# Top-k attention with an MLP behind it: the heads of pairs 1 to 3 loaded by rows and turned on TensorE

## The chip, the cores and the metric

The kernel runs on one core of a Trainium2 chip. The metric is device time in microseconds (us); a time given for a kernel is the median of several runs. One execution of each kernel is also recorded by the hardware profiler; that record is the profile, or the trace. Its engines are TensorE (PE; its weight loads are PEld), VectorE (DVE), ScalarE (ACT), GpSimd (POOL) and SyncE (SP), which here only issues DMAs. ACTq and SPq are DMA issues on the queues of ScalarE and SyncE. An entry such as L331 is a line of the kernel's source.

## The reference

Eight batches of eight heads, 576 positions, 64 values a head, all float32. Each row of scores keeps its 32 largest; the rest is masked out before the softmax. The heads' outputs side by side are the rows x (512 wide) of an MLP with a normalization ahead of it and a residual. The weights arrive as float64, and the kernel converts them to float32 itself.

```python
# attention: q, k, v are (8, 8, 576, 64)
scores = (1 / sqrt(64)) * q @ k^T
kth    = 32nd largest of each row of scores
scores = where(scores >= kth, scores, -1e9)
attn   = softmax(scores);  o = attn @ v
# MLP: x is (8, 576, 512), w_ch1 (512, 2048), w_ch2 (2048, 512)
xn  = (x - mean(x)) / sqrt(var(x) + 1e-6) * g_ln
out = x + relu(xn @ w_ch1) @ w_ch2
```

## The kernel before

**Tiling.** A job is one batch, one pair of heads (two heads of 64 fill the 128 partitions) and a group of query tiles. A query tile is 128 rows; the 576 rows are four whole tiles and a rest of 64. A unit is one query tile of a job for both heads: its scores are 128 x 2 x 576. The first jobs are batch 0 with its pairs 0, 1, 2, 3 and query tiles 0 and 1, so job 0 has units 0 and 1, job 1 has units 2 and 3, and so on; the next four jobs are the same pairs with query tiles 2 and 3. The list `fresh` holds the jobs that meet a batch and pair for the first time; the others get the turned heads back from a copy in DRAM (`keep_heads` stores it, `fetch_heads` loads it).

**Turned heads.** The scores need k and q with the 64 values of a head on the partitions and positions along the row: kT (128 x 576), qT (128 x 256, query tiles 0 and 1) and late_qT (128 x 320, the others). `load` brings k and q so that VectorE's transpose, which works on blocks of 32 x 32, ends in that layout: four DMAs for k and four for q, each with runs of 32 floats, 128 bytes. `turn_heads` (L331) then makes three VectorE transposes. k and q each have a tile of their own (`kin`, `qin`), in a pool with one buffer, so the next job's load waits until these are turned.

**The order.** There are 160 units, and the program is written out step by step; in step n VectorE selects the top values of unit n (four rounds of MAX8 and MATCH_REPLACE8, L447 and L433; `select`) and halves the next unit (L425, L426; `halve`), TensorE makes the scores of unit n + 2 (L404), ScalarE copies them out of PSUM (L385; `take_scores`), ScalarE and GpSimd mask unit n - 1 (L496, then the subtraction L499) and ScalarE takes the exponential (L507). In the first eight steps TensorE then turns that unit's weights in two halves (L565, copied out by ScalarE in L577) and an end piece (L599, L609). A group's values follow (L632, L640; `values`), and `place` puts them into x (L677, L654). Every engine works through its own instructions strictly in program order. A list `todo` holds the MLP's matmuls; each step takes from it in several `fill()` calls what its share allows. The MLP begins at step 9, with its first product on TensorE at 109.7 us.

**The weights.** A piece is 128 x 512 float64, fetched by SyncE (L147) into one of four buffers. ScalarE splits it in three instructions (L163, L165, L168), GpSimd clamps the size and scales the sign (L164, L170), VectorE shifts (L176), and GpSimd joins (L182, L184). Four pieces are split before step 0, then one a step up to step 7 and two a step from step 10.

**Where heads are turned.** The main loop holds a table `turns`: job 1 is turned in step 0, job 2 in step 1, job 3 in step 2, and the next fresh job, of batch 1, in step 12 (its first transpose is at 143.7 us). In a step the turn stands after VectorE's second selection round, and between the first and second half of the unit's turn on TensorE; the load of the next fresh job follows it at once:

```python
        if n in turns:
            turn_heads(turns[n])
            later = fresh.index(turns[n]) + 1
            if later < len(fresh):
                load(fresh[later], nc.sync, nc.sync, n >= EARLY)
        if n == 0:
            scores(units[2])
            take_scores(units[2])
```

Ahead of step 0 stands a start-up: job 0 is loaded and turned, unit 0 scored, job 1 loaded with k on SyncE's queue and q on ScalarE's, unit 1 scored and copied, the norm's gain g brought into place by a small TensorE transpose (L196, copied by L197), and four pieces split. PSUM has eight banks: five for the attention's short results (`brief`) and three for the MLP's products (`product`).

Of the kernel before, what the change touches and what calls it, by code (L numbers as in the profile page):

```python
# [11 lines left out]
FP32 = mybir.dt.float32  # L12
# [9 lines left out]
J = 4  # L22
# [7 lines left out]
def compute(  # L30
# [12 lines left out]
    nc = tc.nc  # L43
    P = nc.NUM_PARTITIONS
    B, H, S, D = q.shape
# [3 lines left out]
    JP = J * P  # L49
    R = S - JP  # L50
    NHP = H // 2
# [5 lines left out]
    def pool(name, bufs, **kw):  # L57
        return ctx.enter_context(tc.tile_pool(name=name, bufs=bufs, **kw))
# [6 lines left out]
    ldpool = pool("ld", 1)  # L65
# [24 lines left out]
    def const(shape, name):  # L90
        return consts.tile(shape, FP32, tag=name, name=name)
# [8 lines left out]
    def product(name):  # L100
        return mmps.tile([P, 512], FP32, tag="mm", name=name)
# [8 lines left out]
    ident = const([P, P], "ident")  # L110
# [90 lines left out]
    queue = list(pieces)  # L201
# [92 lines left out]
    def load(job, first, second, later=False):  # L294

        job.ins = {}
        for name, src, queue in (("k", k, first), ("q", q, second)):
            t = ldpool.tile([P, S], FP32, tag=name + "in", name=name + "in")

            def part(i, t=t, src=src, queue=queue):  # L300
                head, d0 = 2 * job.hp + i * 32 // D, i * 32 % D
                queue.dma_start(
                    t[i * 32 : (i + 1) * 32, :].rearrange("b (n a) -> b n a", a=32),
                    src[job.b, head, :, d0 : d0 + 32].rearrange("(n b) a -> b n a", b=32),
                )

            for i in range(P // 32):
                if later:
                    age = (4 * len(job.ins) + i) // 2
                    loads.add(lambda i=i, part=part: part(i), -age)  # L310
                else:
                    part(i)
            job.ins[name] = t

    def load_values(job):

        job.v = vpool.tile([P, 2 * J + 1, D], FP32, tag="v", name="vb")
        rows = v[job.b, 2 * job.hp : 2 * job.hp + 2].rearrange("h s d -> (h s) d")
        nc.sync.dma_start(job.v[:], rows.rearrange("(c p) d -> p c d", p=P))

    def fill_ends(job):
        for h in range(2):
            r = slice(h * R, (h + 1) * R)
            nc.scalar.copy(ends[r, h * D : (h + 1) * D], job.v[r, J, :])

    def turn_heads(job):
        job.T = {}
        for name in "kq":
            for part, c0, c1 in HEADS[name]:
                t = turned_tile(part, c1 - c0)  # L330
                nc.vector.transpose(t[:], job.ins[name][:, c0:c1])  # L331
                job.T[part] = t
# [3 lines left out]
    def turned_tile(part, width):  # L336
        return kqpool.tile([P, width], FP32, tag=part + "T", name=part + "T")
# [697 lines left out]
    rows, rest = ([0, 1], [2, 3]), [J]  # L1035
# [15 lines left out]
    N = len(units)  # L1051
    END = N + 7

    fresh = []
    for j in jobs:
        j.twin = next((x for x in fresh if (x.b, x.hp) == (j.b, j.hp)), None)
        if j.twin is None:
            fresh.append(j)

    for i, u in enumerate(units):  # L1060
# [58 lines left out]
    def at(i):  # L1119
        return units[i] if 0 <= i < N else None  # L1120
# [76 lines left out]
    def placed_at(u):  # L1197
        return u.i + u.group.lag + 1 if u and u.rest and u.job.b % 2 else None
# [8 lines left out]

    gives_first = min(gives)
    load(fresh[0], nc.sync, nc.scalar)

    nc.scalar.copy(gcol[:], half[:])
    for x in batches[-1]:
        x.fetch()
    turn_heads(fresh[0])
    nc.sync.dma_start(grow[:], g_ln.rearrange("(c p) -> c p", p=P))
    scores(units[0])
    take_scores(units[0])
    load(fresh[1], nc.sync, nc.scalar)
    halve(units[0])
    scores(units[1])  # L1220
# [4 lines left out]
    for n in range(END):  # L1225
# [11 lines left out]
        late = next((x for x in (at(n - 4), at(n - 5)) if placed_at(x) == n), None)  # L1237
# [84 lines left out]
# [5 lines that stand above are left out]
# [3 lines left out]
        for x in (u if n < EARLY else None, mk if n > EARLY else None):  # L1330
            if x and x is units[x.job.last]:
                load_values(x.job)
                ends_due[n + 1] = x.job
# [62 lines left out]
@with_exitstack  # L1396
def kernel(
    ctx: ExitStack,
    tc: tile.TileContext,
    *operands: bass.AP,  # L1400
):
    nc = tc.nc
    doubt = ctx.enter_context(tc.tile_pool(name="doubt", bufs=1)).tile(
        [1, 1], I32, tag="doubt", name="doubt"
    )
    compute(tc, *operands, low_rounds=1, doubt=doubt[:])
    again = nc.values_load(  # L1407
        doubt[:], min_val=0, max_val=1,
        skip_runtime_bounds_check_because="a comparison's result",
    )  # L1410
    with tc.If(again > 0):
        compute(tc, *operands, low_rounds=2, doubt=None)
# [31 lines left out]
```

## Time and profile before

| what | us |
|---|---|
| median of 3 runs | 1595.1 (1593.72 to 1596.26) |
| the profiled execution, its own time | 1593.68 |
| its span | 1591.9 |
| VectorE's head turns (L331), all 32 fresh jobs | 46.9 (x96) |
| VectorE waiting for job 0's first k | 5.6 |

The page cuts the span into 40 slices of 39.8 us each; a digit is the busy share in tenths.

```profile
PE   3578889999999999999999999999999999899997
DVE  6998998999899998989979999999999999657000
ACT  6878887777677777676777776867767766454421
POOL 5968896647474666656656657575757575527614
PEclk6779989999999999999999999999999999999999
DMA  8423641566637754575643675565675555443511
```

The first three slices, up to about 120 us, are the ramp: TensorE is at 3 to 7 tenths and its granted clock (PEclk) below full. From the seventh slice it is at 9 almost everywhere, to the end. VectorE is near full until slice 34, then has no more units to select, and the last 110 us are the MLP on TensorE. The DMA engines are at 8 tenths in the first slice.

### The profile page before, as it was taken

How to read it: one execution, taken by the hardware profiler on the slowest of the kernel's cores; microseconds unless marked ns; L12 is line 12 of the kernel's file. 1: busy time of each engine (PE TensorE's matmuls, PEld its weight loads, DVE VectorE, ACT ScalarE, POOL GpSimd, SP SyncE). 2: the span in 40 equal slices, each digit the busy share in tenths (PEclk: the TensorE clock that was granted, in tenths of full speed). 3: DMA queues.
4: the chain of work that ended last, by engine and by line, in shares of the span. 5: the costliest groups of instructions: out<-in, count | busy, mean ns of one | idle time of the engine just before them, and what ended most of it. 6: DMA issues, size and time to landing. Idle time of an engine off the chain costs nothing. (4 is left out here: it accounts for less than half of the span.)

```text
span 1591.9 us, 27533 instructions
## 1 busy us (share of the span) xinstructions
PE 1478.6 (93%) x8106; PEld 1106.5 (70%) x8106; DVE 1365.4 (86%) x3969; ACT 1085.2 (68%) x3153; POOL 997.5 (63%) x1318
## 2 busy tenths in 40 slices
PE   3578889999999999999999999999999999899997
PEld 2356447567777777777777777777777777688886
DVE  6998998999899998989979999999999999657000
ACT  6878887777677777676777776867767766454421
POOL 5968896647474666656656657575757575527614
PEclk6779989999999999999999999999999999999999
DMA  8423641566637754575643675565675555443511
GB/s 207 125 84 101 156 118 45 147 166 185 176 114 197 193 172 124 160 202 143 200 119 115 180 206 164 151 174 155 186 187 154 169 158 157 139 127 106 140 34 49
DMA packets 381784, 234.21 MB, mean 147 GB/s; under 512 B 262964, under 2 KB 350520, under 8 KB 381624
## 3 DMA queue, kind: packets, MB, share of 16 engines
q1 hardware_dynamic: 376888, 231.76, 52.1%
q8 instruction: 67, 1.10, 0.3%
q10 hardware_dynamic: 4736, 0.59, 0.3%
q14 instruction: 93, 0.76, 0.2%
HBM read 160.43 MB, written 71.83 MB: 146 GB/s over the span
## 5 line engine op out<-in xcount | busy, mean ns | idle before, releaser
L499 POOL TENSOR_TENSOR e<-e,sc 128x576 f32<-128x576 f32 x288 | 413.3, 1454 | 472.9 <-ACT e L496 430.9
L782 PE MATMUL hps<-xT,w 128*128 128x256 f32 x2304 | 539.1, 383 | 2.1 <-ACT xT L744 2.1
L447 DVE MAX8 m<-hi 128x8 f32<-128x296 f32 (+1 forms) x1152 | 471.4, 444 | 1.2
L782 PEld LDWEIGHTS hps<-xT,w 128*128 128x128 f32 x2304 | 426.4, 192 | 65.9 <-issue 11.2
L433 DVE MATCH_REPLACE8 hi<-m,hi 128x288 f32<-128x288 f32 (+1 forms) x864 | 377.2, 441 | 0.0
L496 ACT ACTIVATE e<-sc,m 128x576 f32<-128x576 f32 x288 | 209.3, 769 | 182.0 <-PE scps L599 178.4
L942 PE MATMUL ops<-w,h 128*128 128x256 f32 x1280 | 306.5, 385 | 5.8 <-POOL h L878 3.5
L942 PEld LDWEIGHTS ops<-w,h 128*128 128x128 f32 x1280 | 237.4, 193 | 40.7 <-issue 5.0
L507 ACT ACTIVATE e<-e,m 128x576 f32<-128x576 f32 x288 | 225.4, 785 | 24.5 <-POOL e L499 21.8
L385 ACT COPY sc<-scps 128x288 f32<-128x288 f32 x576 | 187.2, 402 | 42.8 <-POOL e L499 32.5
L439 DVE MAX8 hi<-lo 128x8 f32<-128x288 f32 x288 | 117.8, 444 | 41.3 <-POOL watched L466 41.3
L632 PE MATMUL av<-pt,vb 128*64 128x256 f32 (+2 forms) x1280 | 144.6, 368 | 0.5 <-ACT e L507 0.5
L538 DVE STREAM_TRANSPOSE sc<-e 128x512 f32<-128x512 f32 x174 | 113.6, 685 | 34.6 <-ACT e L507 28.7
L805 ACT ACTIVATE h<-hps 128x512 f32<-128x512 f32 x144 | 87.2, 606 | 77.4 <-PE hps L782 76.9
L425 DVE TENSOR_TENSOR hi<-sc 128x576 f32<-128x576 f32 (+1 forms) x160 | 133.2, 833 | 3.0 <-ACT sc L385 3.0
L426 DVE TENSOR_TENSOR lo<-sc 128x576 f32<-128x576 f32 (+1 forms) x160 | 133.5, 835 | 0.0
L404 PE MATMUL scps<-kT,late_qT 64*128 64x288 f32 (+3 forms) x832 | 122.7, 413 | 0.2 <-ACT pt L577 0.2
L565 PE MATMUL tp<-ident,e 128*128 128x128 f32 x456 | 74.5, 291 | 50.3 <-ACT e L507 30.8
L942 PE MATMUL ops<-wt,s 128*128 128x256 f32 x512 | 118.4, 380 | 0.6 <-POOL s L872 0.6
L632 PEld LDWEIGHTS av<-pt,vb 128*64 128x64 f32 x1280 | 78.3, 138 | 57.5 <-issue 15.6
L404 PE MATMUL scps<-kT,qT 64*128 64x288 f32 x512 | 94.4, 467 | 22.7 <-DVE qT L331 11.2
L565 PEld LDWEIGHTS tp<-ident,e 128*128 128x128 f32 x456 | 57.5, 148 | 77.1 <-ACT e L507 37.5
(107 smaller groups left out, 1910.0 us busy)
## 6 DMA issues: line engine op xcount, KB each, us to landing
turned<-sc SPq DMA_DIRECT2D x87, 512.0 KB, 3.8
pt<-turned SPq DMA_DIRECT2D x348, 128.0 KB, 2.8
w<-forms SPq DMA_DIRECT2D x128, 256.0 KB, 4.6
vb<-in_v_dram SPq DMA_DIRECT2D x80, 288.0 KB, 4.1
raw<-in_moe_w_ch_dram SPq DMA_DIRECT2D x32, 512.0 KB, 4.7
kT<-kept SPq DMA_DIRECT2D x48, 288.0 KB, 3.5
kin<-in_k_dram SPq DMA_DIRECT2D x128, 72.0 KB, 2.7
kept<-kT SPq DMA_DIRECT2D x32, 288.0 KB, 3.2
```

Of the source, the lines that this page charges most:

```text
L385: nc.scalar.copy(u.sc[:, t, s * HALF : (s + 1) * HALF], u.made[s][t][:, 0:HALF])
L404: nc.tensor.matmul(ps[i * R : i * R + ql, o : o + width], qT[r, q0 : q0 + ql], kT[r, k0 : k0 + width], start=True, stop=True,)
L425: nc.vector.tensor_tensor(hi, a, b, ALU.max)
L426: nc.vector.tensor_tensor(lo, a, b, ALU.min)
L433: nc.vector.match_replace(x, m[:, t, :], x, LOWEST)
L447: nc.vector.max(m[:, t, :], u.hi[:, t, 0:width])
L496: nc.scalar.activation(u.e[:, t], u.sc[:, t], AF.Relu, bias=u.edge[:, t : t + 1], scale=-STEEP)
L499: nc.gpsimd.tensor_tensor(u.e[:, t], u.e[:, t], u.sc[:, t], ALU.subtract)
L507: nc.scalar.activation(u.e[:, t], u.e[:, t], AF.Exp, bias=u.bias[:, t : t + 1], scale=-scale, accum_out=g.den[:, col : col + 1],)
L632: nc.tensor.matmul(av[h * D : (h + 1) * D, 0 : g.nq], vb[:, h * (J + 1) + c, :], g.blocks[:, h, 0 : g.nq // 32, c, :], start=(c == 0), sto ...
L782: nc.tensor.matmul(ps[0][:, side * N : (side + 1) * N], w1[:, c, f * P : (f + 1) * P], self.xT[:, c, 0:N], start=(c == 0), stop=(c == NC - 1),
L942: nc.tensor.matmul(bank[name][:, 0:Q], a(j), rhs, start=first and j == 0, stop=(j == G - 1), skip_group_check=not first,)
```

## The change

k and q of a job now share one tile, `raw`. For jobs with `whole` set, which are the second to fourth fresh jobs (batch 0, pairs 1, 2 and 3, turned in steps 0, 1 and 2), the load is by rows: positions on the partitions, in runs of 64 floats (256 bytes), with three DMAs for k and three for q. Nine chunks of 128 x 128 result: four of k, four of q, and one with the last 64 positions of both. `turn_rows` transposes the nine on TensorE into three PSUM banks of the MLP's products, and ScalarE copies them into kT, qT and late_qT in five instructions. Job 0 and all jobs from batch 1 on are loaded and turned as before, but through views of the shared tile. The planner's costs for a step are not changed.

```diff
@@ load
         job.ins = {}
-        for name, src, queue in (("k", k, first), ("q", q, second)):
-            t = ldpool.tile([P, S], FP32, tag=name + "in", name=name + "in")
+        raw = ldpool.tile([P, 2, S], FP32, tag="raw", name="kqin")
+        if job.whole:
+            load_rows(job, raw, first, second)
+            return
+        for s, (name, src, queue) in enumerate((("k", k, first), ("q", q, second))):
+            t = raw[:, s]
...
+    def load_rows(job, raw, first, second):
+        rows = job.rows = raw[:].rearrange("p s n -> p (s n)").rearrange("p (c x) -> p c x", x=P)
+        heads = slice(2 * job.hp, 2 * job.hp + 2)
+        for s, (src, queue) in enumerate(((k, first), (q, second))):
+            for h in range(2):
+                queue.dma_start(
+                    rows[:, s * J : (s + 1) * J, h * D : (h + 1) * D],
+                    src[job.b, 2 * job.hp + h, 0:JP, :].rearrange("(c p) d -> p c d", p=P),
+                )
+            queue.dma_start(
+                rows[s * R : (s + 1) * R, 2 * J].rearrange("p (h d) -> p h d", h=2),
+                src[job.b, heads, JP:S, :].rearrange("h s d -> s h d"),
+            )
...
+    def turn_rows(job):
+        kT, qT, late = (turned_tile(part, w) for part, w in (("k", S), ("q", 2 * P), ("late_q", JP - 2 * P + R)))
+        job.T = {"k": kT, "q": qT, "late_q": late}
+        pss = [product("heads") for _ in range(3)]
+        for j in range(2 * J + 1):
+            ps, c = pss[j // J], j % J
+            nc.tensor.transpose(ps[:, c * P : (c + 1) * P], job.rows[:, j], ident[:])
+        nc.scalar.copy(kT[:, 0:JP], pss[0][:, 0:JP])
+        nc.scalar.copy(qT[:], pss[1][:, 0 : 2 * P])
+        nc.scalar.copy(late[:, 0 : 2 * P], pss[1][:, 2 * P : JP])
+        nc.scalar.copy(kT[:, JP:S], pss[2][:, 0:R])
+        nc.scalar.copy(late[:, 2 * P : 2 * P + R], pss[2][:, R : 2 * R])
+
     def turn_heads(job):
+        if job.whole:
+            turn_rows(job)
+            return
         job.T = {}
...
@@ the list of fresh jobs
-    fresh = []
+    fresh, WHOLE = [], NHP - 1
     for j in jobs:
         j.twin = next((x for x in fresh if (x.b, x.hp) == (j.b, j.hp)), None)
         if j.twin is None:
+            j.whole = 0 < len(fresh) <= WHOLE
             fresh.append(j)
```

## The prediction

> **What bounds the kernel now.** I read the page's busy times first, then the windows cut where the work changes, then the waits of VectorE and GpSimd in the first 101 us, then the timeline of that stretch.
>
> The page says who is full over the whole span; the windows (start:end, length, busy us and instruction count of each engine, granted clock, share of the DMA engines, GB/s) say when.
>
> ```profile
> PE 1478.6 (93%) x8106; PEld 1106.5 (70%) x8106; DVE 1365.4 (86%) x3969; ACT 1085.2 (68%) x3153; POOL 997.5 (63%) x1318
> ...
> 24.40:62.50 38.10, 17.59 (x76) 10.14 (x74) 31.97 (x100) 28.50 (x72) 37.01 (x33) 0.63 0.70 180
> 62.50:101.00 38.50, 26.49 (x141) 17.45 (x141) 38.50 (x115) 33.75 (x95) 34.20 (x32) 0.69 0.28 87
> 240.00:1480.00 1240.00, 1208.92 (x6854) 917.40 (x6853) 1145.77 (x3365) 863.93 (x2592) 754.52 (x1043) 0.99 0.56 158
> ```
>
> From 240 us on TensorE is busy 97.5% of the time: its work there is fixed, so the end moves by what the ramp before it is shortened or lengthened. The change touches only steps 0 to 2 of the ramp (heads of jobs 1, 2, 3 are turned at 16, 28 and 42 us). In 24.4 to 62.5, around them, TensorE is under half busy and GpSimd is busy 37.0 of 38.1 us. VectorE has 6 us free.
>
> VectorE's waits between 16 and 101 us, and its own turn at step 1 in the timeline (start, length, engine, line, operation):
>
> ```profile
> DVE size L176 <- POOL size L164: 6.1, 3, 4.2
> DVE kT L331 <- issue: 0.8, 1, 0.8
> ...
> 28.21 0.76 DVE L331 STREAM_TRANSPOSE kT<-kin 128x576 f32<-128x576 f32 x1
> 28.90 0.40 DVE L331 STREAM_TRANSPOSE qT<-qin 128x256 f32<-128x256 f32 x1
> 29.23 0.46 DVE L331 STREAM_TRANSPOSE late_qT<-qin 128x320 f32<-128x320 f32 x1
> ...
> 38.83 0.61 POOL L164 TENSOR_SCALAR size<-size 128x512 f32<-128x512 f32 x1
> 39.47 0.43 DVE L176 TENSOR_SCALAR size<-size 128x512 uint32<-128x512 uint32 x1 [4.20 <-POOL size L164]
> ```
>
> After its turns VectorE stands still for 4.20 us at 39.47 (again 1.64 at 50.47 and 0.28 at 58.79) until GpSimd's clamp (L164) of a weight piece comes round in GpSimd's order. GpSimd itself has no wait at all between 24.4 and 97.8 us. So in the stretch that the change touches GpSimd is the bound, and VectorE reaches the same points early.
>
> What lets GpSimd begin is ScalarE, which splits five weight pieces of three instructions each:
>
> ```profile
> 11.43 1.49 ACTq L302 DMA_DIRECT2D qin<-in_q_dram  x2
> 12.96 1.31 ACT L385 COPY sc<-scps 128x288 f32<-128x288 f32 x4 [2.89 <-PE tp L196]
> 14.12 0.21 ACT L197 COPY gcol<-tp 128x4 f32<-128x4 f32 x1
> 14.18 0.71 ACT L163 ACTIVATE size<-raw 128x512 f32<-128x512 f32 x1
> ...
> 23.48 0.99 POOL L170 TENSOR_SCALAR sign<-sign,gcol 128x512 f32<-128x512 f32 x1
> 24.44 1.26 POOL L182 TENSOR_TENSOR size<-size,wt 128x512 uint32<-128x512 uint32 x1
> ```
>
> The wait at 12.96 is put down to TensorE, but unit 1's scores were done by 11.1. ScalarE was held by its own queue: it issues the four DMAs of job 1's q, two at 9.27 and 9.62, and the other two only from 11.43 to 12.92. Its copies, gcol and the splits stand behind them.
>
> **What the Trainium skill says.** "Perfetto Trace Analysis", Identifying the Most-Contended Engine: improve the fullest engine, and that can differ by regime. This trace agrees (TensorE over the span, GpSimd here). "SBUF — State Buffer", SBUF: two separate sides: VectorE with two SBUF inputs and GpSimd share a port pair as an exclusive lock. It agrees: GpSimd's join L182 takes 1.26 us alone and 2.49 at 45.88, when VectorE halves a unit (L425, L426; 0.75 each). "DMA: Bandwidth & Descriptors", Why small descriptors are slow (HBM only): each packet has a fixed overhead. It agrees: the packet records show 12.7 ns on average for 128 bytes and 19.0 for 256. "TensorE: Matmul & The Clock Gate", Part 4: PE-mode transpose: the result goes to PSUM and must be copied out; so here, L565 is followed by ScalarE's L577.
>
> **The change part by part.**
>
> VectorE: three turns of 0.78 + 0.40 + 0.47 us go; back to back one takes 1.41 (28.21 to 29.62), 4.2 for three, and the 0.76 wait for job 1's DMA ahead of the first. What is late next is L176: the turns of steps 0 and 1 only lengthen the 4.20 wait, that of step 2 the 1.64 wait. Worth nothing by themselves; were GpSimd not in the way, 5.0.
>
> DMA: a load has 4608 packets of 128 bytes (8 DMAs) and gets 2304 of 256 (6 DMAs). 4608 x 12.7 / 16 engines = 3.7 us, 2304 x 19.0 / 16 = 2.7: 0.9 us less of the DMA engines, three times. Jobs 2 and 3 were loaded well ahead, so this is hidden. Job 1's counts in one place: ScalarE issues three DMAs (32 + 32 + 8 packets an engine) instead of four of 36. Two of 36 were taken at once before, and 72 is the same depth, so I take it that all three go by about 10.5, at the latest just after 11.43. Unit 1's copies then run from 10.5 or 11.8, done by 11.8 or 13.1. The gcol copy next needs g's DMA, which landed for L196 at 12.71 and so sets 13.0. The splits start at 13.0 or 13.1 instead of 14.18: 1.1 us gained (0 if the issue still blocks; 2.2 if g lands earlier with less traffic).
>
> K's DMAs to the shared raw tile wait for all three of job 0's turns: 7.08 instead of 6.38. They queue behind 2 MB of weights anyway: nothing.
>
> The lock: the halve of unit 1 (19.90 to 21.8) made GpSimd's L164/L170 take 1.00, 1.33, 0.99 instead of 0.61, 0.69, 0.69; it finished the fifth piece at 24.4 although ScalarE was done at 22.7. With 1.41 + 0.76 us gone VectorE halves near 17.7, two pieces earlier, and GpSimd has caught up by the fifth, since it needs 1.30 a piece and ScalarE 1.68. Worth up to 0.9, down to -0.5 if a halve falls badly elsewhere; I take 0.9.
>
> TensorE: nine transposes a turn. L565's four take 1.11 us at half clock, so 2.5 us (1.5 at full); its own busy time costs nothing at under half load. But at steps 1 and 2 they stand between the two halves of a unit's turn: L565's second half starts at 35.6 instead of 33.37, and ends and scores behind it. The PSUM banks are the MLP's, free until its first product at 109.7 us.
>
> ScalarE: five copies a turn. By L577 (0.58 for 512 wide), L650 (0.35 for 256) and L609 (0.27 for 128, taken for 64): 1.8 by durations, about 1.4 in a row, as four L385 of 0.41 take 1.3. In step 0 they follow the fifth split (21.4 in place of 22.6); unit 2's scores come after them, so mask 0 starts about 0.5 us later than at 24.04, and GpSimd wants it at 29.65: hidden. Step 1, on the old clock: second half of the turn copied by 37.5, mask 1 from 37.9 (was 35.41), its first half done at 38.6, wanted at 40.43: hidden; the next split ends at 42.3, and exp, free to go at 41.86, is 0.45 late. Step 2 repeats it: mask 2 from 49.2, wanted at 51.42; exp 0.85 late at 53.7. From 55 to 92 ScalarE has no idle time to win that back. There each mask's first half is done some 0.8 us before GpSimd's subtraction (first mask begins 65.94, so 66.7 against 67.50). So 0.85 leaves 0.05 to 0.1 late: I charge 0.1. Bounds: 0 to 3.6 (below, slower).
>
> SP: the next load waits for TensorE's ninth transpose, about 35.7 instead of 29.00 in step 1 and 46 instead of 42.91 in step 2. Behind it stand v, the kept heads and a weight fetch (34.98, then near 40), which ScalarE splits at 48.81; a fetch lands in 5.2 (median): hidden with 2 to 3 us left. Gone, if the transposes run late.
>
> Later jobs keep VectorE's turns; only their tile is shared, and their DMAs are issued after all three turns. Nothing.
>
> Sum: -1.1 - 0.9 + 0.1 = -1.9, and about -0.2 for ScalarE's shorter first queue and the three loads' lighter traffic: -2.1. The profiled execution took 1593.68 (span 1591.9 and 1.8 around it), so 1591.6 for it; the median of three runs is 1.4 above it, so 1593.0.
>
> **The rivals.**
> A, the above: the earlier start of GpSimd's chain, 1593.0 (1591.0 to 1594.4 from the bounds).
> B, VectorE's time does count: from 59 to 101 it has no idle time either, and GpSimd's own times are stretched by its halves; if VectorE running ahead moves halves out of GpSimd's way step after step, the 4.2 + 0.8 come through: 1590.1. Against it: GpSimd's row of instructions has no gap for VectorE to close.
> C, nothing moves: g's landing or the q issue still sets 14.18, the lock falls as before: 1595.0.
> D, slower: ScalarE's lateness passes its 0.8 us of slack. The place is steps 1 and 2, where the copies and the nine transposes stand ahead of the second half of the turn; L565's longest was 477 ns, nine of these are 4.3 us, 1.8 more, in both steps: 0.85 + 3.6 = 4.45 late, less 0.8 = 3.6 on GpSimd's chain to 95 us. With the start gained it is +1.6, without it +3.6: 1598.5. It decides from 2.8 us of lateness (0.8 slack, 2.0 gain).
>
> **How the numbers follow.** What a measurement of this kernel can tell from none is about 0.2%, 3.2 us. A 0.52 (0.20 of it beyond 3.2 us, since several gains were taken at their lower ends), B 0.25 (0.24 beyond), C 0.06, D 0.17 (0.15 beyond). Faster 0.44, within 0.41, slower 0.15. Predicted 1593.0, as A is likeliest. Range: B's lower part below 1589.0 and D's upper above 1597.0 hold about 2 in 10 between them, so 1589.0 to 1597.0.
>
> **What would show it.** ScalarE's first split near 13.0; GpSimd's first join near 22.4; still no wait of GpSimd from there to its gap near 96; VectorE's wait at L176 grown from 4.2 to about 6; exp waiting less for GpSimd in steps 2 and 3. Wrong: first split at 14.2 (C), a wait of L499 on L496 between 38 and 95 us (D), or GpSimd's chain shorter by more than its start moved (B).

## The result and the profile after

The changed kernel took 1592.2 us (median of 20 runs, 1589.0 to 1593.6), the kernel before in the same session 1594.6 (20 runs, 1590.5 to 1596.3): a ratio of 0.9985, with a 95% interval from 0.9979 to 0.9991. That is 2.4 us less, between 1.4 and 3.3. 1593.0 had been predicted, with a range from 1589.0 to 1597.0.

The profiled execution of after is the lowest of its 20 runs, 1589.0 (span 1587.2), 4.7 below that of before. The first page line and the windows at the places shown of before (start:end, length, busy us and instruction count of PE, PEld, DVE, ACT and POOL, granted clock, share of the DMA engines, GB/s):

```profile
PE 1474.1 (93%) x8133; PEld 1106.5 (70%) x8133; DVE 1363.1 (86%) x3960; ACT 1090.4 (69%) x3168; POOL 1000.8 (63%) x1318
```

```profile
24.40:62.50 38.10, 19.40 (x102) 13.82 (x100) 30.46 (x91) 33.05 (x89) 37.01 (x33) 0.72 0.62 169
62.50:101.00 38.50, 25.75 (x141) 17.04 (x140) 38.50 (x113) 33.52 (x93) 33.93 (x30) 0.78 0.29 88
240.00:1480.00 1240.00, 1208.18 (x6870) 917.66 (x6869) 1148.29 (x3368) 866.13 (x2596) 756.24 (x1043) 1.00 0.56 158
```

The page has nine VectorE instructions less and 27 TensorE instructions and 15 ScalarE instructions more: three turns of three, nine and five, as the diff says. In 24.4 to 62.5 VectorE is busy 1.5 us less, ScalarE 4.6 more, and GpSimd exactly as long as it was: 37.01 us in 33 instructions, in both kernels. In the third window TensorE's busy time is the same to 0.7 us in 1209. The granted clock of the first window is 0.72 for 0.63 before. In the twelve profiles of this study in which GpSimd's work is as it was, it is 0.59 to 0.63 where VectorE turns all heads and 0.68 to 0.76 where TensorE turns some; GpSimd's row of instructions is not shorter for it, as the section on the prediction shows.

**Where the 4.7 us between the two profiles are.** I set each MAX8 of VectorE in after beside the same one in before, since they mark the progress of the 160 units. At 90 us after leads by 0.3 us; from 117 to 655 us, but for a few instructions, it stands between 0.04 ahead and 0.5 us behind. The lead of 3.3 us at the last MAX8 comes in three steps, near 656, 1329 and 1390 us; the other 1.4 us lie behind the last compute instruction, at the very end. The first of the steps in the windows, of before and then of after (the granted clock is the third number from the end):

```profile
656.00:662.00 6.00, 5.63 (x26) 3.65 (x28) 6.00 (x20) 3.07 (x13) 0.00 (x0) 0.72 0.67 213
```

```profile
656.00:662.00 6.00, 5.13 (x35) 3.26 (x36) 6.00 (x19) 3.57 (x14) 0.00 (x0) 1.00 0.51 151
```

The steps are stretches of some 3.4 us in which TensorE is granted half its clock. Before has one at 656 and one at 1329 us where after has none, and two in a row at 1390 where after has one; each is worth 1.2 to 1.3 us, and all are far from any changed line. In all fourteen profiles each stretch after 250 us begins within 1.6 us of the end of one of TensorE's pauses of 1.7 to 3.5 us, which stand at the same five places of the program (near 560, 655, 747, 1325 and 1388 us). Whether a pause is followed by one differs from profile to profile (3.4 to 13.6 us of them in all). At 656 us, in before and then in after, the pause is the same and the same six matmuls follow:

```profile
656.37 2.92 PE L942 MATMUL ops<-w,h 128*128 128x256 f32 x6 [1.97 <-ACT o L907]
```

```profile
656.87 1.56 PE L976 MATMUL ops<-w,h 128*128 128x256 f32 x6 [2.00 <-ACT o L941]
```

So this pair of single executions can't say what the change brought. The medians can; the first 100 us show what it did there.

**The ramp of after.** ScalarE, up to the first split (start, length, engine, line, operation, idle time before it and what ended it):

```profile
9.95 0.43 ACTq L324 DMA_DIRECT2D kqin<-in_q_dram  x1
...
10.42 0.73 ACTq L324 DMA_DIRECT2D kqin<-in_q_dram  x1
11.19 0.68 ACTq L328 DMA_DIRECT2D kqin<-in_q_dram  x1
11.91 1.31 ACT L419 COPY sc<-scps 128x288 f32<-128x288 f32 x4 [1.32 <-PE scps L438]
13.08 0.20 ACT L197 COPY gcol<-tp 128x4 f32<-128x4 f32 x1
13.13 0.72 ACT L163 ACTIVATE size<-raw 128x512 f32<-128x512 f32 x1
```

Three DMAs instead of four; the copies begin at 11.91 instead of 12.96 and the first split at 13.13 instead of 14.18. That much came as foreseen. Then VectorE and GpSimd up to the first join:

```profile
18.19 0.74 DVE L459 TENSOR_TENSOR hi<-sc 128x576 f32<-128x576 f32 x1
...
18.42 2.74 POOL L170 TENSOR_SCALAR sign<-sign,gcol 128x512 f32<-128x512 f32 x1 [0.26 <-ACT sign L168]
...
18.85 0.75 DVE L460 TENSOR_TENSOR lo<-sc 128x576 f32<-128x576 f32 x1
...
19.52 1.09 DVE L176 TENSOR_SCALAR size<-size 128x512 uint32<-128x512 uint32 x3
...
21.24 0.61 POOL L164 TENSOR_SCALAR size<-size 128x512 f32<-128x512 f32 x1
...
21.89 0.43 DVE L176 TENSOR_SCALAR size<-size 128x512 uint32<-128x512 uint32 x1 [1.29 <-POOL size L164]
...
24.33 1.43 POOL L182 TENSOR_TENSOR size<-size,wt 128x512 uint32<-128x512 uint32 x1
```

GpSimd's L170, 0.69 us alone, took 2.74, and the next instruction on GpSimd does start 2.8 us later. VectorE, with no turn to do, ran the halve (L459, L460) and three shifts of weight pieces (L176) in one row from 18.19 to 20.6, and GpSimd came in only when VectorE had to wait for it. So the first join stands at 24.33, 0.1 us earlier than before, although the first split came 1.05 earlier.

From there the waits of VectorE from 16 to 101 us in after, and of ScalarE from 20 to 60 us in after and then in before (line, what it waited for: us in total, times, longest):

```profile
DVE size L176 <- POOL size L164: 8.9, 4, 5.7
```

```profile
ACT e L541 <- POOL e L533: 4.2, 6, 1.4
```

```profile
ACT e L507 <- POOL e L499: 8.6, 6, 2.7
```

The time that VectorE no longer needs has gone into its wait for GpSimd: 8.9 us instead of 6.1, the longest 5.7 instead of 4.2. ScalarE's exponential still waits for GpSimd, 4.2 us instead of 8.6: its extra copies have filled idle time. And GpSimd's subtraction of unit 7, the end of the ramp for it, in before and in after:

```profile
92.14 2.95 POOL L499 TENSOR_TENSOR e<-e,sc 128x576 f32<-128x576 f32 x2
```

```profile
91.86 2.95 POOL L533 TENSOR_TENSOR e<-e,sc 128x576 f32<-128x576 f32 x2
```

From first join to the end of that line before needs 70.6 us and after 70.5.

### The profile page after: what moved, and what is told of

Its sections match the earlier page's. It is cut to its first block, busy times and chain, and to the rows that moved or that the text cites. A ratio compares the mean times of both kernels' runs of the same rounds, so it can differ in the third digit from the quotient of the medians.

```text
span 1587.2 us, 27565 instructions
## 1 busy us (share of the span) xinstructions
PE 1474.1 (93%) x8133; PEld 1106.5 (70%) x8133; DVE 1363.1 (86%) x3960; ACT 1090.4 (69%) x3168; POOL 1000.8 (63%) x1318
## 4 chain that ended last, share of the span: by engine, by line
PE 56%; DVE 27%; ACT 8%; POOL 5%; DMA 2%; issue 2%; SPq 1%; ACTq 0%; DVEq 0%; POOLq 0%
PE hps L816 22%; PE ops L976 15%; DVE m L481 8%; DVE hi L467 7%; PE scps L438 6%; PE av L666 5%; DVE sc L572 3%; DVE lo L460 2%; DVE hi L459 2%; DVE hi L473 2%; PE tp L599 2%; ACT e L530 2%; POOL e L533 2%; PE ops L855 2%; ACT sc L419 1%
## 5 line engine op out<-in xcount | busy, mean ns | idle before, releaser
L816 PEld LDWEIGHTS hps<-xT,w 128*128 128x128 f32 x2304 | 425.5, 192 | 65.6 <-issue 11.2
L460 DVE TENSOR_TENSOR lo<-sc 128x576 f32<-128x576 f32 (+1 forms) x160 | 137.8, 861 | 0.0
L459 DVE TENSOR_TENSOR hi<-sc 128x576 f32<-128x576 f32 (+1 forms) x160 | 131.5, 822 | 3.0 <-ACT sc L419 3.0
```

The costliest lines, as they stand in the source:

```text
L459: nc.vector.tensor_tensor(hi, a, b, ALU.max)
L460: nc.vector.tensor_tensor(lo, a, b, ALU.min)
L816: nc.tensor.matmul(ps[0][:, side * N : (side + 1) * N], w1[:, c, f * P : (f + 1) * P], self.xT[:, c, 0:N], start=(c == 0), stop=(c == NC - 1),
```

## The experiments

All were timed beside the kernel before; a ratio is time over the time of before in the same session (its median was 1591.4, 1593.9 and 1593.1 us in the three sessions). My theory at the outset: GpSimd's row of instructions bounds the ramp, VectorE's time is worth nothing, and what is gained is the earlier start of that row. The rival: VectorE's time counts.

**r_before and r_after: both kernels again.** Unchanged sources.

> The kernel before once more, unchanged, as the measure of what a measurement can tell: ratio 1.000 with an interval of about 0.001 to either side. In its profile GpSimd's row of instructions should again begin with the first join (L182) near 24.4 us and run without a wait to about 97.8. If the late difference between the two first profiles (three stretches of 3.4 us at half TensorE clock after 650 us) is chance, this profile has another number of them and its span differs by about 1.2 us for each.

> The changed kernel once more, unchanged: ratio 0.9985. Theory (the lock took the gain): the splits begin near 13.1 again, GpSimd's third L170 is stretched to about 2.7 by VectorE's halve and shifts, and the first join begins at 24.3, so units are no earlier than before at 100 us. Rival (the first profile was an unlucky one): L170 is not stretched here, the first join begins at 22.4 to 23.4 and the units at 100 us are 1 to 2 us earlier than before.

Measured: before against itself 1593.1 us, ratio 1.0003 (0.9992 to 1.0013); after 1588.4, ratio 0.9982 (0.9973 to 0.9990). The gain stands, and one comparison is good to about 1 in 1000, 1.6 us. The new profile of before was as useful as a warning: its first split fell at 15.01 and its first join at 26.31, 1.9 us later than in the first profile of the same source. The start-up alone moves by that much from one execution to the next. In the new profile of after L170 is stretched again (2.73 us) as the theory had it; the first split is at 12.48 and the first join at 23.62, so this execution is 1.0 us ahead of before at 100 us, as the rival had it.

**e_vec_back and e_vec_back0: VectorE's work put back, for nothing.** After, with VectorE's three transposes of the same sizes at the end of each turn, or in step 0 alone. They are additional work; nobody reads what they write.

```diff
+        job.raw = raw
...
+        scrap = w2[:, NF - 2 : NF].rearrange("p f n -> p (f n)")
+        for s, c0, c1 in ((0, 0, S), (1, 0, 2 * P), (1, 2 * P, S)):
+            nc.vector.transpose(scrap[:, c0:c1], job.raw[:, s, c0:c1])
```

e_vec_back0 has `if job is fresh[1]:` ahead of the loop.

> The changed kernel, with VectorE's three transposes of each turn put back as work for nothing (from the raw tile into a part of w2 that is not yet written; the result is not used). Theory (GpSimd's row is the bound, VectorE's time costs nothing): no slower than the changed kernel; the halve of unit 1 falls later, off the third L170, the first join begins near 23.4 instead of 24.3, and the time is 1591.3 (0.9 below the changed kernel), between 1590.3 and 1592.7. Rival (VectorE's 4.2 us were the gain): 1596.4, ratio above 1.000. Rival (only the load's form counts): equal to the changed kernel within 0.5.

> The changed kernel, with VectorE's three transposes put back for nothing in step 0 alone (job 1). Theory: all of the shift of the halve of unit 1 is in this step, so first join and time are as with all three put back, within 0.5 us: near 23.4 and 1591.3. Rival (VectorE's time counts): a third of 4.2 us lost, 1593.6.

Measured: 1588.7 us, ratio 0.9985 (0.9976 to 0.9993), and 1588.9, ratio 0.9981 (0.9973 to 0.9990). Beside r_after's 0.9982 neither has lost anything: 4.9 us of VectorE work in the ramp (three turns of 1.65; one of them in e_vec_back0) cost nothing that can be seen. Two such ratios can be told apart from some 2 us on: that rules out the 4.9 us as the gain, while e_vec_back0 alone would not rule out its 1.65. The rival, that VectorE's time was the gain, falls. What didn't come as expected is the lock. I had thought that a later halve would avoid the long L170 and the first join would stand near 23.4; it came at 25.35 in e_vec_back and 24.76 in e_vec_back0. In e_vec_back's timeline L170 met the row of five just so:

```profile
19.21 0.75 DVE L463 TENSOR_TENSOR hi<-sc 128x576 f32<-128x576 f32 x1
19.31 2.88 POOL L170 TENSOR_SCALAR sign<-sign,gcol 128x512 f32<-128x512 f32 x1 [0.28 <-ACT sign L168]
...
20.54 1.10 DVE L176 TENSOR_SCALAR size<-size 128x512 uint32<-128x512 uint32 x3
```

So the long block is not made by the removal of VectorE's turn. r_before has it too (2.85 us), with the turn in place. In all of these three finished pieces stood ready, so that three shifts followed the halve without a wait.

**e_q_sync: only the queue of job 1's q changed, on the kernel before.**

```diff
-    load(fresh[1], nc.sync, nc.scalar)
+    load(fresh[1], nc.sync, nc.sync)
```

> The kernel before, with the four DMAs of job 1's q issued on SyncE's queue instead of ScalarE's; VectorE turns all heads as before. Theory (the gain is ScalarE's queue ahead of the splits): ScalarE's copies of unit 1 and the splits begin at about 13.0, set by g, instead of 14.2 and 15.0 in the two profiles of before, the first join follows some 11 us later (24 to 24.5 instead of 24.4 and 26.3), and the ratio is about 0.9985, as for the changed kernel. Rival (the loads by rows or the turns on TensorE bring it): the ratio is 1.000.

Measured: 1590.7 us, ratio 0.9984 (0.9976 to 0.9993). One word brings as much as the whole change, with every turn on VectorE. ScalarE's timeline:

```profile
10.86 1.00 ACT L385 COPY sc<-scps 128x288 f32<-128x288 f32 x3 [0.50 <-PE scps L404]
12.63 0.16 ACT L197 COPY gcol<-tp 128x4 f32<-128x4 f32 x1 [0.76 <-PE tp L196]
12.69 0.67 ACT L163 ACTIVATE size<-raw 128x512 f32<-128x512 f32 x1
```

With no DMA to issue, ScalarE has its copies done at 11.9, a microsecond before the kernel before begins the last four. Now the wait for g's transpose shows (0.76 us at 12.63), and the first split is at 12.69. The hold on ScalarE was its own DMA issue.

How the earlier split becomes a shorter run this profile doesn't show. GpSimd lost the lead again ahead of the first join, and it ends unit 7 no earlier than in before:

```profile
21.16 2.59 POOL L164 TENSOR_SCALAR size<-size 128x512 f32<-128x512 f32 x1 [0.87 <-ACT size L163]
24.50 1.26 POOL L182 TENSOR_TENSOR size<-size,wt 128x512 uint32<-128x512 uint32 x1
92.23 2.96 POOL L499 TENSOR_TENSOR e<-e,sc 128x576 f32<-128x576 f32 x2
```

**e_job1 and e_jobs23: the change in parts.** After with `WHOLE = 1` (job 1 by rows, jobs 2 and 3 turned by VectorE), and after with job 1 left out:

```diff
-            j.whole = 0 < len(fresh) <= WHOLE
+            j.whole = 1 < len(fresh) <= WHOLE
```

> The changed kernel with job 1 alone loaded by rows and turned on TensorE; jobs 2 and 3 go back to 128-byte loads and VectorE. Theory: the gain hangs on job 1's q on ScalarE's queue, so the ratio is that of the changed kernel, 0.9983, and the splits begin between 12.5 and 13.1. Rival (all three jobs share the gain): a third of it, 0.9994.

> The changed kernel with job 1 loaded and turned as before, jobs 2 and 3 by rows and TensorE. Theory: ScalarE is held by job 1's q as before, the splits begin at 14.2 to 15.0, the ratio is 1.000 (0.999 to 1.001). Rival (all three jobs share the gain): two thirds of it, 0.9988.

Measured: 1590.9 us, ratio 0.9979 (0.9969 to 0.9990), and 1591.4, ratio 0.9985 (0.9978 to 0.9992). Job 1 alone brings as much as all three, as expected. That jobs 2 and 3 alone bring as much was not: I had expected 1.000. Their start was late, as it should be with four DMAs of q on ScalarE:

```profile
9.90 3.27 ACTq L306 DMA_DIRECT2D kqin<-in_q_dram  x3
...
14.43 0.71 ACT L163 ACTIVATE size<-raw 128x512 f32<-128x512 f32 x1
```

The first join is at 24.49 and the row to unit 7 70.3 us long. By first split, first join and row this profile can't be told from that of before, and yet the runs are faster: the earlier first split can't be the only gain. Taken at their middles the two parts sum to 5.7 us where the whole brings 2.4 to 2.9; at the near ends of their intervals (1.6 and 1.3) they would fit it.

**e_shared: only the shared tile.** After with `WHOLE = 0`: every job is turned by VectorE; what is left of the change is one tile for k and q, so that the next load waits for all three transposes.

> The changed kernel with no job loaded by rows: every head turned by VectorE as before, only the shared tile is left, so job 1's k is issued after all three of job 0's turns (about 0.8 us later). Theory (rows for jobs 2 and 3 do count for something, since jobs 2 and 3 alone gave 0.9985): ratio 1.000. Rival (jobs 2 and 3 gain only by what they have in common with this kernel, the later k): ratio 0.9985, first join after the first split by about 10, VectorE's turn of job 1 without its wait.

Measured: 1592.3 us, ratio 0.9992 (0.9983 to 1.0001). It lies between, and its interval takes in both no change and the 0.9985 of e_jobs23. If it is real, half of e_jobs23's gain comes from the later loads and not from TensorE's turns; this run doesn't settle it.

**e_early: the start made earlier still.** After, with job 1's q on SyncE and g's DMA ahead of the four weight fetches.

```diff
     nc.scalar.copy(gcol[:], half[:])
+    nc.sync.dma_start(grow[:], g_ln.rearrange("(c p) -> c p", p=P))
     for x in batches[-1]:
         x.fetch()
     turn_heads(fresh[0])
-    nc.sync.dma_start(grow[:], g_ln.rearrange("(c p) -> c p", p=P))
...
-    load(fresh[1], nc.sync, nc.scalar)
+    load(fresh[1], nc.sync, nc.sync)
```

> The changed kernel, with job 1's q on SyncE's queue too and the DMA of g ahead of the four weight pieces. Theory: with neither in the way ScalarE copies unit 1 as soon as TensorE has made it (about 10.8) and splits from 12.0, 0.5 to 1.1 earlier than in the two profiles of the changed kernel; the first join and the units at 95 us move by the same, ratio 0.9977 (1591.4 becomes 1587.8). Rival (something behind the splits, the lock or the weights' landing, sets the first join): splits earlier, the join not, ratio 0.9983 as for the changed kernel.

Measured: 1589.3 us, ratio 0.9967 (0.9955 to 0.9979, from six runs), by that about 5.3 us less than before. The first split is at 11.57, the first join at 23.03, and GpSimd ends unit 7 at 93.50, the earliest of all. It is the best version of the study; its interval touches that of r_after, so that it beats the change itself is likely, not shown.

**e_halve_early: the halve moved away from the shifts.** After, with the first `halve` ahead of the turn and so ahead of the shifts.

```diff
+        if n == 0:
+            halve(nxt)
         if n in turns:
...
-        if nxt:
+        if nxt and n:
             halve(nxt)
```

> The changed kernel with VectorE's halve of unit 1 moved up in step 0, ahead of its third selection round. Theory (the port pair's lock eats the earlier start): no GpSimd instruction between the first and fifth split is stretched beyond 1.6 us, the first join comes 10.0 to 10.5 us after the first split instead of 11.1 to 11.4, and the time is 0.8 us below the changed kernel's: ratio 0.9978. Rival (the lock is not what separates splits and join): 11.2, ratio 0.9983.

Measured: 1591.1 us, ratio 0.9984 (0.9976 to 0.9991). The lock went as expected:

```profile
15.21 0.85 DVE L459 TENSOR_TENSOR hi<-sc 128x576 f32<-128x576 f32 x1
...
15.99 1.30 POOL L170 TENSOR_SCALAR sign<-sign,gcol 128x512 f32<-128x512 f32 x1 [0.54 <-ACT sign L168]
...
19.01 1.83 DVE L176 TENSOR_SCALAR size<-size 128x512 uint32<-128x512 uint32 x3
...
23.77 1.43 POOL L182 TENSOR_TENSOR size<-size,wt 128x512 uint32<-128x512 uint32 x1
```

No GpSimd instruction before the first join took over 1.30 us, and from first split (14.05) to first join it took 9.7 us, against 11.2 in after. So the long block is gone in this profile, with the halve moved. Which feature of the row made it is not shown by this: here the halve also began while GpSimd was in the middle of an instruction, and that alone goes with short blocks in other profiles (the lock, in the next section). Nor is a gain of time shown: 0.9984 where 0.9978 was expected, both inside the interval.

**e_clamp and e_clamp_vec: work taken from GpSimd.** If GpSimd is the bound, VectorE's spare time should be worth something once GpSimd's work is put there. The clamp L164 of the first eight pieces goes to VectorE, just ahead of the shift; with it e_early's start, the early halve, and two of the first four pieces shifted after the halve and two after the third selection round. e_clamp is made from after, e_clamp_vec in the same way from before, with VectorE's turns.

```diff
-            nc.gpsimd.tensor_scalar(size_f, size_f, HIGH_MAX, HIGH_MIN, ALU.min, ALU.max)
+            if i >= CLAMPED:
+                nc.gpsimd.tensor_scalar(size_f, size_f, HIGH_MAX, HIGH_MIN, ALU.min, ALU.max)
...
         def shift(self):
+            if self.i < CLAMPED:
+                size_f = self.size.bitcast(FP32)
+                nc.vector.tensor_scalar(size_f, size_f, HIGH_MAX, HIGH_MIN, ALU.min, ALU.max)
...
+    CLAMPED = 8
```

> The changed kernel with q of job 1 on SyncE's queue, g loaded ahead of the weights, the halve of unit 1 moved up, and the clamp (L164) of the first eight weight pieces moved from GpSimd to VectorE, just ahead of its shift. Theory (GpSimd's row is the ramp): first split at 11.6 to 12.0, first join near 21.5, the 70.5 us of GpSimd from the first join to its gap near 95 shorter by three clamps of 0.7, about 68.4; units at 95 us 4 us earlier than in the changed kernel, ratio 0.9955. Rival (ScalarE, nearly full with the head copies, or VectorE becomes the bound): the row gets waits, gain 1 to 2 us only, ratio 0.997.

> The same four edits on the kernel before, so with VectorE turning all heads. Theory: VectorE has 6 us to spare in the ramp and ScalarE is free of the head copies, so it comes to within 1 us of the kernel with the same edits on top of the change: ratio 0.9955 to 0.9965. Rival (turns on TensorE are needed for this to pay): VectorE, with clamps and turns, holds GpSimd up, ratio 0.998 or more.

Measured: 1592.3 us, ratio 0.9995 (0.9987 to 1.0004), and 1596.3, ratio 1.0023 (1.0015 to 1.0031). The first join of e_clamp came at 21.52, as hoped; but its row to unit 7 then took 73.9 us instead of 70.5. The waits from 20 to 101 us, of e_clamp and then of e_clamp_vec:

```profile
POOL e L538 <- ACT e L535: 9.0, 5, 2.5
ACT m L498 <- DVE m L486: 4.6, 6, 1.1
```

```profile
POOL e L504 <- ACT e L501: 8.9, 5, 2.5
ACT m L464 <- DVE m L452: 6.4, 7, 1.9
```

GpSimd now stands still for 9 us, for ScalarE's mask, and ScalarE in turn waits for VectorE's selection; VectorE has no wait at all from 16 to 101 us in either profile. It has become the bound. Here the turn counts: with it on VectorE the same kernel is 2.8 parts in 1000 slower than without. e_clamp_vec also waits 2.4 us for a weight fetch that stands behind q on SyncE's queue, so not all of that is VectorE's time.

## Why the prediction came out right, and where it did not

**The bound.** Shown. Across the twelve profiles in which GpSimd's work is as it was, its row from first join to the end of unit 7 is 70.3 to 70.8 us long, whoever turns the heads. So far case A's reason holds; that an earlier start of this row is what shortens the whole run is a further step, taken up under the sum.

**VectorE worth nothing.** Shown by e_vec_back and e_vec_back0: the 4.9 and 1.65 us put back cost nothing that the runs can tell, which is less than some 2 us. The longest wait at L176 went to 5.7, where about 6 was given. It counts only when VectorE is filled otherwise (e_clamp_vec).

**ScalarE's queue, 1.1 us.** Shown for the first split, and of the size given. First split in the six profiles with job 1 by rows and q still on ScalarE: 12.5 to 14.1, mean 13.4; in the four with VectorE's layout there: 14.2 to 15.0, mean 14.5. With no q on that queue at all it is 12.7, or 11.6 to 12.0 with g earlier too. Whether the third DMA would still block had been left open, and it goes both ways. In r_after it was through at 11.2, in e_halve_early it began only at 12.10, which is the scatter of 12.5 to 14.1.

**The lock, 0.9 us: the step that failed.** I had written that with the halve two pieces earlier "GpSimd has caught up by the fifth". The halve did come earlier, at 18.19, but three finished pieces stood ready behind it to be shifted, and the five VectorE instructions kept GpSimd out for 2 us in one piece. From first split to first join it took 11.2 us instead of 10.26: 0.9 lost, where 0.9 was to be won. "First join near 22.4" became 24.33. I had counted the halve's two instructions as blockers, and not the shifts, which I knew only as waiting. The Trainium skill, "SBUF — State Buffer", SBUF: two separate sides, says that an instruction of one engine holds the pair to its end and that the other blocks; here VectorE kept it through five instructions in a row.

Nor is this a fixed cost of the change: r_before has it too, at 2.85 us. And the row alone doesn't make it. In before a halve and four shifts follow each other as closely, and the two engines take turns:

```profile
19.45 0.69 POOL L170 TENSOR_SCALAR sign<-sign,gcol 128x512 f32<-128x512 f32 x1 [0.29 <-ACT sign L168]
19.90 0.85 DVE L425 TENSOR_TENSOR hi<-sc 128x576 f32<-128x576 f32 x1
20.22 1.00 POOL L164 TENSOR_SCALAR size<-size 128x512 f32<-128x512 f32 x1
20.67 1.16 DVE L426 TENSOR_TENSOR lo<-sc 128x576 f32<-128x576 f32 x1
21.31 1.33 POOL L170 TENSOR_SCALAR sign<-sign,gcol 128x512 f32<-128x512 f32 x1
21.75 2.25 DVE L176 TENSOR_SCALAR size<-size 128x512 uint32<-128x512 uint32 x4
```

Here GpSimd was in the middle of an instruction when the halve began. That is so in four of the twelve profiles with GpSimd's work as it was (before, e_shared, e_jobs23, e_halve_early), and their longest L164 or L170 ahead of the first join is 1.3 to 1.5 us. In the other eight GpSimd stood between two instructions at that moment (in e_early the next had begun 0.05 us earlier), and the longest is 2.2 to 2.9. So it seems to hang on which engine is at work within a tenth of a us, which can change from one execution to the next. No run was made to test that.

**ScalarE's lateness, +0.1 us, and rival D.** Over-estimated and harmless. The nine transposes of steps 1 and 2 took 2.10 and 2.08 us, not 2.5, and the exponential that was to be 0.45 and 0.85 us late still waits for GpSimd in all three steps, 4.2 us in six waits. Rival D needed 2.8 us of lateness; there was none.

**SyncE.** As worked out: the loads are issued at 35.56 and 45.82, for 35.7 and 46 predicted, and no weight piece came late.

**The sum.** It was 2.1, and 2.4 was measured (1.4 to 3.3): 0.15% of the time, inside the 0.2% to which the prediction gave 0.41, and not beyond it on the fast side, to which it gave 0.44. The agreement is luck in part, since the terms are not those of the sum: without the 0.9 of the lock 1.2 is left, and the runs found more. Nor do the profiles show how the start reaches the end. GpSimd ends unit 7 at 95.5 us on average in the four profiles with VectorE's layout for job 1 and its q on ScalarE's queue, and at 94.9 in the six with rows: 0.6 earlier, most of it because r_before, at 96.7, is one of the four. In e_q_sync it is 95.2 and in e_vec_back 95.8, later than the 95.1 of before, and the runs of both have the full gain.

A MAX8 that before reaches at 242 us, when the MLP's start lies behind, doesn't settle it. Beside the first profile of before, r_before and e_shared are 3.1 and 1.9 us late there and e_early is 1.2 early; six others stand between 0.6 early and 0.2 late. But e_job1 and e_vec_back, 1.8 and 1.5 late, were not slower in their runs. The profiled execution of e_job1 was the slowest of its twelve. It lost its time between 90 and 129 us, where TensorE's clock is still changing: the stretch at half clock that begins between 105 and 109 us is 10.2 us long in r_before, e_shared and e_job1, and 6.8 in the other eleven profiles. The windows show it, in before and then in e_job1 (0.92 and 0.86 granted):

```profile
101.00:143.00 42.00, 35.13 (x182) 26.16 (x180) 32.91 (x91) 33.71 (x83) 28.15 (x30) 0.92 0.27 75
```

```profile
101.00:143.00 42.00, 35.34 (x177) 25.50 (x174) 30.18 (x85) 32.98 (x82) 27.12 (x28) 0.86 0.27 75
```

These are single executions, and their scatter is as large as the effect. Whether part of the gain is that the changed kernels meet the long stretch less often is a rival that no run tests.

**What stays open.** By which path the 2.4 us come: that job 1's q off ScalarE's queue brings as much as the change is shown (e_q_sync), that the earlier start of GpSimd's row carries it to the end is not. What jobs 2 and 3 bring when job 1 is as it was (2.4 us, from 1.3 to 3.5), and whether it adds to what job 1 brings. e_shared leaves it open whether the shared tile is part of it. Each comparison is uncertain by about 1.3 us. Foreseen rightly were that VectorE's time is worth nothing, that ScalarE's queue held the splits by 1.1 us, and the row of GpSimd that nothing in the change shortens.

## What to carry to other kernels

Before moving work off an engine, look at what its idle time waits for: here VectorE already waited for GpSimd, and 4.9 us given back to it changed nothing, while one word that took four DMA issues off ScalarE's queue gave as much as the whole change. Where two engines share a port pair, count every instruction that the freed engine will run back to back and not only those that stood there before, and don't book a gain that hangs on which of the two comes first by a tenth of a us. And where the effect is a few us in 1600, take the size from medians and let the profile say only where, against more than one profile of the same kernel.

## What was not expected of the hardware

- ScalarE's DMA issues held its computing. It took two of job 1's q DMAs at once and was then held until the others had gone in (12.92 in before, 11.87 in after), with scores waiting that TensorE had finished by 11.1 and 11.6. Without these issues its copies were done at 11.9.
- VectorE's halve and the shifts behind it kept GpSimd's 0.69-us instruction out until it had taken 2.7 to 2.9 us, in four of the fourteen profiles; in four more it was the clamp L164, 0.61 alone, that took 2.2 to 2.9. Between one and four shifts followed the halve without a pause in these eight. In the three profiles in which the halve began while GpSimd was at work and four shifts followed it, the two took turns, and nothing took over 1.5 us.
- In a kernel whose TensorE is 97% busy from 240 to 1480 us, TensorE's pauses of 1.7 to 3.5 us are followed by 3.4 or 6.8 us at half clock in some executions and not in others, at 1.2 to 1.3 us for each 3.4. They made a difference of 3.3 us between two profiles, more than the change.
